# Regrouping the V rounds of a one-token attention kernel: waits between runs of rounds, and spare matmuls moved from the rounds to the tail

## The chip, the cores and the metric

One core of one Trainium2 chip. The metric is device time in microseconds of one execution; medians of several executions are given with their range, or with the interval of a ratio. "Span" is the time from the first to the last instruction of the profiled execution; it is about 1.4 us shorter than the time in most runs (2.8 us in the profiled run of the kernel before: 659.01 and 656.2).

## The reference, cut to what matters

One token (512 numbers) goes through layer norm, attention over a cache of 65,536 positions (8 K/V heads of 128, each serving 4 query heads), an output projection, a second layer norm and a gated feed-forward block, all in bf16:

```python
scores = jnp.einsum("bhqd,bhkd->bhqk", q, k) * (Dh ** -0.5)
p = _softmax(scores, axis=-1)
o = jnp.einsum("bhqk,bhkd->bhqd", p, v)
...
h = x + (o.transpose(0, 2, 1, 3).reshape(B, Sq, Hq * Dh) @ wo)
h2 = h + _B_ref(_layernorm(h), w_gate, w_up, w_down)
```

Everything is read once. K and V are 268.4 MB of the 282.33 MB that the profile counts, so this is a streaming kernel with little arithmetic for each byte.

## The kernel before

SyncE issues the loads, one after another on one queue, into a ring in SBUF. K of a head comes in three loads (12, 8 and 12 chunks of 512 KB), V the same. DVE transposes K's chunks, PE makes the scores, ACT the exponentials, and PE multiplies them with V in **rounds**: eight matmuls, 32 output rows each, on four column groups of the array. A head has a run of 10 rounds beside its first scoring block and one of 6 after its last. SyncE's loads wait for these rounds, because they free ring space:

```python
for h in range(1, HKV):
    load("K", h, 0, ["F0.1" if h == 1 else f"F{h - 1}.3"], "ka", f"K{h}.0")
    load("V", h - 1, 0, ["F0.3" if h == 1 else f"PV{h - 2}.3:2"], "va", f"V{h - 1}.0")
    load("V", h - 1, 1, ["F0.4" if h == 1 else f"PV{h - 2}.3"], "vb", f"V{h - 1}.1")
    load("K", h, 1, [f"F{h}.0"], "ka", f"K{h}.1")
    load("K", h, 2, [f"F{h}.1", f"PV{h - 1}.0:4"], "kb", f"K{h}.2")
    load("V", h - 1, 2, [f"PV{h - 1}.0"], "vb", f"V{h - 1}.2")
# ... last head: V7.0, output weights wo, V7.1, V7.2, V7.2b, gate, up, down weights
```

PE's program is a loop of registers and branches. This is the round (cut):

```python
label("values", "part")
e.reg_mov(m, PARTS[0])                 # 10 rounds; 6 in the last part
warm(e, 3)                             # three spare matmuls, results unused
# ...
goto("sums", "values")
pv_regs(e)                             # addresses of the round
# ...
away("br_eq", p, c, "waits", waits, "products")   # test in every round: time to wait for V?
goto("products", "sums")
section("B")                           # eight matmuls
mm_at(e, ps(5, 0, 504, 96, 128), ..., kept=True)  # the spare matmul of the round
# ... step p, v, m
e.br_ne(m, 0, on_true="sums", on_false="sums_end")
```

The waits for V's next piece stand off the loop ("away"): after 6 of the 10 rounds, and in the last head after 4 of the 6. Spare matmuls are there to keep PE's array busy and its granted clock up: the mean clock was 0.872 with them.

Of the kernel before, what the change touches and what calls it, by code (L numbers as in the profile page):

```python
# [10 lines left out]
ALU = mybir.AluOpType  # L11
# [15 lines left out]
PT_ROW = 4 * 512 + 8  # L27
# [8 lines left out]
class Prog:  # L36
# [14 lines left out]
    def op(self, eng, fn, deps=(), name=None, to=None, times=1):  # L51
        assert name is None or name not in self.where, name
        self.ops[eng].append(dict(fn=fn, deps=[d for d in deps if d], name=name, dma=None, to=to, times=times, part=self.part.get(eng)))
        if name:
            self.where[name] = (eng, len(self.ops[eng]) - 1)
# [160 lines left out]
def bass_sequential_preLN__gqa_block_cached__glu_gated_glu__decode_kernel(  # L216
# [21 lines left out]
    with ExitStack() as es:  # L238
        def sb(name, shape, dt):
            return es.enter_context(nc.sbuf_tensor(name, shape, dt))  # L240
# [18 lines left out]
        PT_sb = sb("PT_sb", [128, PT_ROW], bf16)  # L259
        qz = sb("qz", [128, 8 * 64], bf16)  # L260
# [39 lines left out]
        def ps(bank, c0, c1, p0=0, p1=128):  # L300
            return PS[p0:p1, bank * 512 + c0: bank * 512 + c1]
# [5 lines left out]
        op, dma = P.op, P.dma  # L307
# [98 lines left out]
        def addr_of(t, elements=0):  # L406
            return nc.lookup_mloc(t).addr + 2 * elements

        def at_reg(t, reg, ap):
            return mybir.RegisterAccessPattern(ap=ap, dtype=bf16, memsetref=t.name + "_set", regref=reg.name, is_regloc_offset=False,  # L410
                                               reg_ap_offset=reg.name, const_ap_offset=0, const_sub_tensor_id=0)

        def mm_at(e, out, lhsT, rhs, start, cols, col0=0, kept=False):
            more = dict(ldweights=False) if kept else {}
            return e.add_instruction(mybir.InstMatmult(  # L415
                name=nc.get_next_instruction_name(), engine=mybir.EngineType.PE, ins=[rhs, lhsT], outs=[e.lower_ap(out)],
                start_tensor_calc=start, stop_tensor_calc=False, tile_size=(128, cols), tile_position=(0, col0),
                bass_skip_group_check=True, **more))

        def warm(e, n=1, load=True):  # L420
            for i in range(n):
                more = dict(ldweights=False) if i or not load else {}
                e.add_instruction(mybir.InstMatmult(  # L423
                    name=nc.get_next_instruction_name(), engine=mybir.EngineType.PE, ins=[e.lower_ap(qz[:, 0:504]), e.lower_ap(ident[:, :])],
                    outs=[e.lower_ap(ps(5, 0, 504))], start_tensor_calc=True, stop_tensor_calc=True, tile_size=(128, 128),
                    tile_position=(0, 0), bass_skip_group_check=True, **more))

        regs, R, here = [], {}, OrderedEngineSet([mybir.EngineType.PE])
# [3 lines left out]
        def label(name, under=None):  # L432
            under = under or blocks[-1][0] if blocks else None
            parent = dict(blocks)[under] if under else "default"
            blocks.append((name, nc.switch_body(name, parent=parent, valid_engines=here)))

        def goto(name, under=None):
            nc.br(name, engines=here)
            label(name, under)

        def reg(e, i):
            while len(regs) <= i:
                regs.append(e.alloc_register(f"a{len(regs)}"))
            return regs[i]
# [133 lines left out]
        PARTS = {0: 10, 3: 6}  # L578
# [83 lines left out]
        def pe_flow(e, section):  # L662
            later = []

            def away(op, reg_, value, name, body, back=None):
                getattr(e, op)(reg_, value, on_true=name, on_false=f"{name}_not")
                later.append((name, body, back or f"{name}_not", blocks[-1][0]))
                label(f"{name}_not")

            i, w, p, v, m, c, s = (R.setdefault(n, e.alloc_register(f"r_{n}")) for n in "iwpvmcs")  # L670
            w0, p0 = addr_of(ktw, W0 + NC - 1 + 127), addr_of(PT_sb, 31 * 4)
            v_at = [addr_of(ring, j * CH) for j in AT["V"]]
            step = (2 * 2 * 512, 2 - 2 * 2 * 512)
            lag = v_at[0] - addr_of(ring, AT["V7"][0] * CH)
            i_last = v_at[0] - lag
            i_first = i_last + HKV * lag
            e.reg_mov(i, i_first)
            e.reg_mov(s, step[0])
            goto("head")
            e.reg_mov(w, w0)  # L680
            e.reg_mov(p, p0)
            e.reg_mov(c, p0 + 6)
            e.reg_alu(v, i, v_at[0], ALU.min)
            goto("part")
            e.br_eq(i, i_last, on_true="values", on_false="scores")
            label("scores")
            for half in range(NC // NR):
                for je in range(4):
                    if half or je:
                        e.reg_alu(reg(e, half * 4 + je), w, 2 * (je * WJ - half), ALU.add)  # L690
            away("br_eq", w, w0, "first_scores", lambda: section("As"), "more_scores")
            section("An")
            goto("more_scores", "scores")
            section("A")
            e.br_eq(i, i_first, on_true="next", on_false="values")
            label("values", "part")
            e.reg_mov(m, PARTS[0])
            warm(e, 3)
            away("br_eq", w, w0, "values0", lambda: section("V0"), "sums")
            e.br_ne(w, w0 - 12, on_true="next", on_false="values3")  # L700
            label("values3")
            e.reg_mov(v, v_at[2])
            e.reg_mov(m, PARTS[3])
            section("V3")
            goto("sums", "values")
            pv_regs(e)

            def last_second():
                section("L")

            def waits():
                e.reg_alu(c, c, 8, ALU.add)
                e.br_eq(w, w0, on_true="second", on_false="fourth")
                label("second", "waits")
                away("br_eq", i, i_last, "rows_of_o", last_second, "products")
                section("V2")
                nc.br("products", engines=here)
                label("fourth", "waits")
                e.br_ne(i, i_last, on_true="products", on_false="last_rounds")
                label("last_rounds", "fourth")  # L720
                section("VL")

            away("br_eq", p, c, "waits", waits, "products")
            goto("products", "sums")
            section("B")
            mm_at(e, ps(5, 0, 504, 96, 128), at_reg(PT_sb, reg(e, 11), [[PT_ROW, 128], [4, 32]]), e.lower_ap(qz[:, 0:504]), True, 32, 96, kept=True)
            e.reg_alu(p, p, s, ALU.add)
            e.reg_alu(s, s, step[0] ^ step[1], ALU.bitwise_xor)
            e.reg_alu(v, v, 2 * 2 * CH, ALU.add)
            e.reg_alu(m, m, -1, ALU.add)  # L730
            e.br_ne(m, 0, on_true="sums", on_false="sums_end")
            label("sums_end")
            def outs():
                warm(e, 2)
                section("O")
                warm(e, 1, load=False)

            away("br_eq", w, w0 - 12, "outs", outs)
            goto("next", "part")
            e.reg_alu(w, w, -4, ALU.add)  # L740
            e.br_ne(w, w0 - 16, on_true="part", on_false="head_end")
            label("head_end")
            e.br_eq(i, i_last, on_true="after", on_false="more_heads")
            label("more_heads")
            section("X")
            e.reg_alu(i, i, -lag, ALU.add)
            nc.br("head", engines=here)
            for name, body, back, under in later:
                label(name, under)
                body()  # L750
                nc.br(back, engines=here)
            label("after", "head_end")
# [44 lines left out]
        P.part = {}  # L797
        regroup(1)
        project(range(NQ - GS, NQ), O3, ["O3.1", "wo1"], last=True)
        op("pe", lambda e: warm(e, 1, load=False))  # L800


        ln_stats(1, lambda e: e.tensor_tensor(hT[1][:, :], ps(YT, 0, 4), x_col[:, :], ALU.add), "yT", STB, 0)
# [72 lines left out]
```

## Time and profile before

| | before |
|---|---|
| time, median of 6 runs | 657.81 us (657.55 to 658.58) |
| span of the profiled run | 656.2 us |
| PE, DVE, ACT busy | 460.9, 350.2, 42.9 us |
| mean granted clock of PE | 0.872 |
| transfer rate up to 653.6 us | 432 GB/s |

These are the lines on PE from the page: first busy time, share of the span and number of instructions for each engine; then three of the costliest groups, with busy time and mean ns of one before the second bar, and the engine's idle time ahead of them after it.

```profile
PE 460.9 (70%) x2564; PEld 73.8 (11%) x1587; DVE 350.2 (53%) x432; ACT 42.9 (7%) x114; POOL 3.6 (1%) x17
...
L415 PE MATMUL PS<-ring,PT_sb 128*32 x1024 | 90.5, 423 | 52.6 <-PEq L171 26.8
...
L415 PE MATMUL PS<-qz,PT_sb 128*32 128x504 bf16 x128 | 53.1, 415 | 0.0
...
L423 PE MATMUL PS<-qz,ident 128*128 128x504 bf16 x121 | 33.7, 374 | 2.1 <-issue 2.1
```

The reader is to see the 1024 V matmuls (128 rounds of 8), the 128 spare matmuls in the rounds, the 121 outside them: PE is busy for 70% of the span.

### The profile page before, as it was taken

What the parts mean: (1) busy time and instruction counts of PE and PEld (TensorE: products, weight loads), DVE (VectorE), ACT (ScalarE), POOL (GpSimd) and SP (SyncE); (2) the same over time, 40 slices, a digit from 0 to 9 for tenths busy, and PEclk for the clock granted to TensorE, in tenths of its full rate; (3) what the DMA queues carried; (4) which work ended last, traced back from release to release, by engine and by line L of the source; (5) the groups of instructions that cost most, each with busy time, mean ns of one, the idle gap of its engine ahead of it and who ended that gap; (6) DMA issues with size and microseconds to landing.
All of it is one profiled execution on the core that took longest, in us unless ns stands there. A gap on an engine that the chain in (4) does not pass through costs nothing.

```text
span 656.2 us, 6578 instructions
## 1 busy us (share of the span) xinstructions
PE 460.9 (70%) x2564; PEld 73.8 (11%) x1587; DVE 350.2 (53%) x432; ACT 42.9 (7%) x114; POOL 3.6 (1%) x17
## 2 busy tenths in 40 slices
PE   0688587857669567786677676695767966777776
PEld 0200010011001010010100111010100101001122
DVE  1299846747266645647258380684536572573202
ACT  1100200020000200001000200002000020001001
POOL 1000000000000000000000000000000000000000
PEclk9989799788889697896887988787978978879798
DMA  9999999999999999999999999999999999999998
GB/s 400 431 447 431 425 421 431 431 437 433 455 431 431 431 415 434 440 443 433 421 447 431 431 423 447 446 434 437 399 447 431 431 431 431 460 434 411 425 429 348
DMA packets 8498, 282.33 MB, mean 430 GB/s; under 512 B 1073, under 2 KB 1074, under 8 KB 1586
## 3 DMA queue, kind: packets, MB, share of 16 engines
q1 hardware_dynamic: 8354, 282.33, 99.6%
q10 hardware_dynamic: 144, 0.00, 0.0%
HBM read 282.33 MB, written 0.00 MB: 430 GB/s over the span
## 4 chain that ended last, share of the span: by engine, by line
DMA 54%; PE 26%; DVE 12%; issue 6%; ACT 1%; PEldq 0%; PEld 0%; SPq 0%
DMA ring<-in_A_k_cache_dram 33%; PE PS L415 22%; DMA ring<-in_A_v_cache_dram 19%; DVE ktw L504 11%; DMA x_col<-in_A_x_dram 2%; PE PS L423 2%; ACT P_sb L550 1%; PE PS L817 0%; DVE PT_sb L560 0%; DVE M_sb L511 0%; PE PS L660 0%; PEldq L171 0%; PE PS L835 0%; PE PS L386 0%; PE PS L544 0%
## 5 line engine op out<-in xcount | busy, mean ns | idle before, releaser
L504 DVE STREAM_TRANSPOSE ktw<-ring 128x1024 f32<-128x1024 f32 x256 | 292.3, 1207 | 152.2 <-DMA ring<-in_A_k_cache_dram 152.2
L415 PE MATMUL PS<-ktw 128*128 128x512 bf16 x1024 | 287.1, 430 | 103.2 <-DVE ktw L504 86.0
L415 PE MATMUL PS<-ring,PT_sb 128*32 x1024 | 90.5, 423 | 52.6 <-PEq L171 26.8
L415 PEld LDWEIGHTS PS<-ktw 128*128 x256 | 26.7, 104 | 343.6 <-issue 246.4
L415 PE MATMUL PS<-qz,PT_sb 128*32 128x504 bf16 x128 | 53.1, 415 | 0.0
L415 PEld LDWEIGHTS PS<-ring,PT_sb 128*32 x1024 | 25.0, 115 | 134.7 <-issue 131.0
L593 ACT ACTIVATE po_sb<-PS,rl 128x512 bf16<-128x512 f32 x8 | 5.5, 687 | 524.1 <-PE PS L415 524.1
L423 PE MATMUL PS<-qz,ident 128*128 128x504 bf16 x121 | 33.7, 374 | 2.1 <-issue 2.1
L511 DVE TENSOR_REDUCE M_sb<-PS 128x1 f32<-128x512 f32 x32 | 19.9, 683 | 22.4 <-PE PS L415 22.4
L539 DVE TENSOR_REDUCE gmj<-PS 1x4 f32<-1x128 f32 x8 | 2.2, 279 | 46.0 <-PE PS L537 46.0
L550 ACT ACTIVATE P_sb<-PS,negmax 128x512 bf16<-128x512 f32 x32 | 21.6, 686 | 0.3
L560 DVE STREAM_TRANSPOSE PT_sb<-P_sb 128x512 bf16<-128x512 bf16 x32 | 20.1, 680 | 1.5 <-ACT P_sb L550 1.5
L386 PE MATMUL PS<-st,onesf 128*128 128x2 f32 x4 | 1.0, 312 | 17.1 <-DVE st L385 17.1
L415 PE MATMUL PS<-ring,xz 128*8 x32 | 9.6, 471 | 2.3 <-issue 2.3
L609 DVE TENSOR_TENSOR Lw<-O,blk_of 128x896 bf16<-128x896 bf16 (+1 forms) x2 | 1.4, 683 | 17.7 <-ACT O L599 17.7
L567 DVE TENSOR_REDUCE lsum<-PS 128x1 f32<-128x4 f32 x8 | 1.3, 162 | 17.6 <-PE PS L565 17.6
L415 PE MATMUL PS<-ktw,O 128*1 x26 | 7.5, 377 | 0.6
L423 PEld LDWEIGHTS PS<-qz,ident 128*128 128x128 bf16 x40 | 3.8, 96 | 35.3 <-issue 35.3
L544 PE MATMUL PS<-one_f,gmrep 1*128 1x1 f32 x16 | 3.2, 268 | 5.0 <-DVE gmrep L541 5.0
L468 DVE STREAM_TRANSPOSE qt<-qh 32x512 bf16<-32x512 bf16 x1 | 0.7, 700 | 11.0 <-ACT qh L465 11.0
L401 DVE CAST hT<-x_col 128x4 f32<-128x4 bf16 x1 | 0.2, 170 | 11.9 <-DMA x_col<-in_A_x_dram 11.9
L550 ACT ACTIVATION_READ_ACCUMULATOR P_sb<-PS,negmax 128x1 f32 x32 | 6.5, 203 | 0.0
(85 smaller groups left out, 73.9 us busy)
## 6 DMA issues: line engine op xcount, KB each, us to landing
ring<-in_A_k_cache_dram SPq DMA_DIRECT2D x16, 6144.0 KB, 24.4
ring<-in_A_v_cache_dram SPq DMA_DIRECT2D x15, 6144.0 KB, 24.9
ring<-in_A_v_cache_dram SPq DMA_DIRECT2D x9, 4096.0 KB, 29.6
ring<-in_A_k_cache_dram SPq DMA_DIRECT2D x8, 4096.0 KB, 24.7
ring<-in_A_wq_dram SPq DMA_DIRECT2D x1, 4096.0 KB, 12.3
ktw<-in_A_wo_dram SPq DMA_DIRECT2D x1, 3584.0 KB, 13.1
ring<-in_A_v_cache_dram SPq DMA_DIRECT2D x1, 2048.0 KB, 36.8
ring<-in_B_w_gate_dram SPq DMA_DIRECT2D x1, 1792.0 KB, 28.4
```

What stands on the lines that cost most here:

```text
L386: op("pe", lambda e: e.matmul(ps(bank, c0, c0 + 2), lhsT=onesf[:, :], rhs=st[i][:, :], start=True, stop=True), [f"st.{i}", f"sta.{i}", "on ...
L415: return e.add_instruction(mybir.InstMatmult(name=nc.get_next_instruction_name(), engine=mybir.EngineType.PE, ins=[rhs, lhsT], outs=[e.low ...
L423: e.add_instruction(mybir.InstMatmult(name=nc.get_next_instruction_name(), engine=mybir.EngineType.PE, ins=[e.lower_ap(qz[:, 0:504]), e.lo ...
L504: op("dve", lambda e, d=dst, sr=src: e.transpose(d, sr), deps, f"T{b}.{c}", to="T")
L511: op("dve", lambda e, u=u: e.tensor_reduce(M_sb[:, u % 4:u % 4 + 1], ps(u % NS, 0, 512), AX.X, ALU.max), [f"S{b}.{NC - NR + k}"], f"mx{u}" ...
L539: op("dve", lambda e: e.tensor_reduce(gmj[:, :], ps(MISC, 0, 128, 0, 1).rearrange("p (i a c) -> p a i c", a=4, c=NC), AX.XY, ALU.max), [f" ...
L544: op("pe", lambda e: e.matmul(ps(MISC, 128, 129), lhsT=gmrep[0:1, :], rhs=one_f[0:1, 0:1], start=True, stop=True), [f"gmrep{h}"], f"neg{h}")
L550: op("act", lambda e, b=b: e.activation(P_sb[:, (b % 4) * 512:(b % 4 + 1) * 512], ps(b % NS, 0, 512), AF.Exp, bias=negmax[:, k:k + 1], sca ...
L560: op("dve", lambda e, b=b: e.transpose(PT_sb[:, (b % 4) * 512:(b % 4 + 1) * 512], P_sb[:, (b % 4) * 512:(b % 4 + 1) * 512]), [f"E{b}"], f" ...
L567: op("dve", lambda e: e.tensor_reduce(lsum[:, :], ps(MISC, 132, 136), AX.X, ALU.add), [f"l{h}"], f"ls{h}", to="D")
L593: op("act", lambda e: e.activation(po_sb[:, :], ps(PO, 0, 512), AF.Copy, scale=rl[:, :]), [f"PV{h}.{NR - 1}", f"rl{h}"], f"po{h}", to="po")
L609: op("dve", lambda e: e.tensor_tensor(Lw[i][:, :].rearrange("p (j c) -> p j c", j=n), bass.AP(tensor=O2, offset=j0, ap=[[NQ, 128], [1, n], ...
```

## The change

Its intent: a round costs PE's sequencer a test and a jump (0.10 to 0.15 us by runs 2 and 5 below) that matter only twice a head. So the rounds are put in runs (6 then 4, and 4 then 2), with the wait between the runs; the spare matmul leaves the round; the parts keep two spares instead of three, and two places in the tail get one more.

```diff
-            e.reg_mov(m, PARTS[0])
-            warm(e, 3)
+            e.reg_mov(m, 6)
+            e.reg_mov(k, 4)
+            warm(e, 2)
 ...
-            e.reg_mov(m, PARTS[3])
+            e.reg_mov(m, 4)
+            e.reg_mov(k, 2)
 ...
             def waits():
-                e.reg_alu(c, c, 8, ALU.add)
+                e.reg_alu(m, k, 0, ALU.add)
+                e.reg_mov(k, 0)
 ...
-            away("br_eq", p, c, "waits", waits, "products")
-            goto("products", "sums")
             section("B")
-            mm_at(e, ps(5, 0, 504, 96, 128), ..., kept=True)
 ...
             e.br_ne(m, 0, on_true="sums", on_false="sums_end")
             label("sums_end")
+            away("br_ne", k, 0, "waits", waits, "sums")
 ...
-                warm(e, 1, load=False)          # after a head's outputs
+                warm(e, 2, load=False)
 ...
-        op("pe", lambda e: warm(e, 1, load=False))   # tail, before the second layer norm
+        op("pe", lambda e: warm(e, 2, load=False))
```

More of the change, by code (lines that the diff above doesn't have):

```diff
@@ L668, in away @@
                 label(f"{name}_not")
-            i, w, p, v, m, c, s = (R.setdefault(n, e.alloc_register(f"r_{n}")) for n in "iwpvmcs")
+            i, w, p, v, m, k, s = (R.setdefault(n, e.alloc_register(f"r_{n}")) for n in "iwpvmks")
             w0, p0 = addr_of(ktw, W0 + NC - 1 + 127), addr_of(PT_sb, 31 * 4)
@@ L681, in pe_flow @@
             e.reg_mov(p, p0)
-            e.reg_mov(c, p0 + 6)
             e.reg_alu(v, i, v_at[0], ALU.min)
@@ L711, in waits @@
             def waits():
-                e.reg_alu(c, c, 8, ALU.add)
+                e.reg_alu(m, k, 0, ALU.add)
+                e.reg_mov(k, 0)
                 e.br_eq(w, w0, on_true="second", on_false="fourth")
                 label("second", "waits")
-                away("br_eq", i, i_last, "rows_of_o", last_second, "products")
+                away("br_eq", i, i_last, "rows_of_o", last_second, "sums")
                 section("V2")
-                nc.br("products", engines=here)
+                nc.br("sums", engines=here)
                 label("fourth", "waits")
-                e.br_ne(i, i_last, on_true="products", on_false="last_rounds")
+                e.br_ne(i, i_last, on_true="sums", on_false="last_rounds")
                 label("last_rounds", "fourth")
                 section("VL")
-            away("br_eq", p, c, "waits", waits, "products")
-            goto("products", "sums")
             section("B")
-            mm_at(e, ps(5, 0, 504, 96, 128), at_reg(PT_sb, reg(e, 11), [[PT_ROW, 128], [4, 32]]), e.lower_ap(qz[:, 0:504]), True, 32, 96, kept=True)
             e.reg_alu(p, p, s, ALU.add)
```

## The prediction

Passages of the recorded text are cut, and each cut is marked: figures and rules of the hardware that no trace or run of this case shows, and a remark on the transfer rate. One is a term of the round's sum, what I took for the test and the jump. With it and the 0.03 us for the spare the sum came to 0.19 us a round, 24 us in all; it stands as my estimate, and so do the numbers that rest on it (0.95 us a round, 3 us in the last head, 1.4 us at the eviction). For the figures of the second rival the trace of the kernel before has: scoring matmuls start 0.43 us apart at a granted clock of 0.50 (77.55 to 81.82 us) and 0.22 us apart at 1.00; the eight matmuls of a round start in two groups of four (639.70 and 639.94 us); eight transposes take 9.13 us (from 529.75 us).

> **What bounds the kernel now.** I read the page's slices and DMA totals first, then the loads from issue to landing, then the last microseconds in stretches, and the rounds that the change edits last.
>
> From the page, slices of DMA share and GB/s and the total:
>
> ```profile
> DMA  9999999999999999999999999999999999999998
> DMA packets 8498, 282.33 MB, mean 430 GB/s; under 512 B 1073, under 2 KB 1074, under 8 KB 1586
> ```
>
> The queue has no slack slice. Split where the data ends (columns: stretch, its length, PE, PEld, DVE, ACT, POOL busy with counts, clock, DMA share, GB/s):
>
> ```profile
> 0.00:653.60 653.60, 460.25 (x2536) 73.43 (x1563) 349.69 (x430) 42.35 (x112) 3.59 (x17) 0.87 1.00 432
> 653.60:656.20 2.60, 0.66 (x44) 0.41 (x32) 0.56 (x2) 0.54 (x2) 0.00 (x0) 0.98 0.00 0
> ```
>
> For 653.6 us the engines run at share 1.00 and 432 GB/s, and only 2.6 us follow. 282.33 MB / 432 GB/s is 653.5 us: the transfers are the time. The chain of waits hides this a little, because it credits PE and DVE with pieces that run beside transfers; it still gives DMA most:
>
> ```profile
> DMA 54%; PE 26%; DVE 12%; issue 6%; ACT 1%; PEldq 0%; PEld 0%; SPq 0%
> ```
>
> Next, whether PE can starve the queue. PE's V rounds release ring space, so loads wait for them. From issue to landing:
>
> ```profile
> ring<-in_A_k_cache_dram SPq DMA_DIRECT2D x16, 6144.0 KB, 24.4
> ring<-in_A_v_cache_dram SPq DMA_DIRECT2D x15, 6144.0 KB, 24.9
> ring<-in_A_v_cache_dram SPq DMA_DIRECT2D x9, 4096.0 KB, 29.6
> ring<-in_A_k_cache_dram SPq DMA_DIRECT2D x8, 4096.0 KB, 24.7
> ...
> ktw<-in_A_wo_dram SPq DMA_DIRECT2D x1, 3584.0 KB, 13.1
> ```
>
> At 432 GB/s a load of 6144 KB needs 14.6 us itself, 4096 KB 9.7 us, 3584 KB 8.5 us. So at its issue there lay ahead of it, as an estimate from these medians, 9.8, 10.3, 19.9, 15.0 and, at the thinnest place (the first output weights, issued at 602.50), 4.6 us of other transfers. A load issued earlier only stands longer in line. DVE waits 152.2 us for K in all, 19 us a head: compute, too, has slack in each head.
>
> Last, the end. The last weights are three loads issued at 618.23, 618.70 and about 619.17, landing after 33.9, 34.6 and 34.8 us: at 652.1, 653.3 and 654.0. The last 56 matmuls use 32, 16 and 8 of their instructions on these three. Weight loads of that line in stretches of 0.05 us (columns: stretch, length, PEld busy and count, clock, DMA share, GB/s):
>
> ```profile
> 653.80:653.85 0.05, 0.05 (x8) 1.00 0.00 0
> 653.85:653.90 0.05, 0.05 (x4) 1.00 0.00 0
> 653.90:653.95 0.05, 0.00 (x1) 1.00 0.00 0
> 653.95:654.00 0.05, 0.03 (x8) 1.00 0.00 0
> 654.00:654.05 0.05, 0.05 (x8) 1.00 0.00 0
> ```
>
> The stream, some 9 active in each stretch, pauses at 653.90 to 653.95 and resumes with exactly eight: the last eight waited for the last load. The chain view calls this whole group PE work behind DVE, but the pause says that the last landing, not PE, sets the end already.
>
> [...] no record shows one branch, only the gaps in which they lie. [...] granted clock 1.00 at 640 to 649 with spare matmuls in every round, 0.50 at 650 to 652.
>
> **The change part by part.** There are 16 V rounds a head (10 in one run, 6 in another), 128 in all. One late round in the trace:
>
> ```profile
> 639.70 0.63 PE L415 MATMUL PS<-ring,PT_sb 128*32 x8 [0.32 <-issue]
> 640.16 0.38 PE L415 MATMUL PS<-qz,PT_sb 128*32 128x504 bf16 x1
> 640.81 0.63 PE L415 MATMUL PS<-ring,PT_sb 128*32 x8 [0.27 <-issue]
> ```
>
> The period is 1.11 to 1.17 us; the eight real matmuls with their loads and the spare are handed over in the first 0.46 us, and the rest is register work and branches. The idle is put down to issue: a round is bound by PE's sequencer, not by the array.
>
> - Removed per round: the spare matmul (about 0.03 us of issue by 17 instructions in 0.46 us; 0.84 - 0.63 = 0.21 us of array time), one compare-and-branch and one jump [...]. Estimate: 1.13 becomes about 0.95 us, so 0.19 x 128 = 24 us less PE time in all.
> - Moved: the test for a wait now stands after a run of 6 or 4 rounds. The runs are 6+4 and 4+2, just where the counter's test fired before (after 6 of 10, and after 4 of the other 6), so each wait covers the same data. The detour stays: the gap before the round at 642.85 was 1.19 us against about 0.3, and I leave its 0.9 us in.
> - Removed per part: one of three spare matmuls, 32 times, about 0.21 us each of array time. Added: one more after each head's output (8) and one in the tail (1), about 0.2 us each, under waits of PE for ACT and DVE. Spare matmuls of that line go from 121 to 64 + 32 + 2 = 98.
> - Array busy time: 460.9 - 128 x 0.21 - 23 x 0.21 = about 429 us if the clock holds.
>
> Of the 24 us, the seven heads before the last give nothing: earlier releases lengthen the line at the queue. In the last head 16 rounds x 0.19 is 3 us at most. There V's pieces land, by issue plus time to landing, at about 626.5, 636 and 641.1 us, queued long before and untouched by PE. I expect the last V rounds to stand at the wait for 641.1 for a moment, so that the final eviction, at 644.72 before, starts near 643.3: some 1.4 us gained. Then the gate and up weights (last piece at 617.75 + 31.9 = 649.7) hold their last matmuls, and finally the down weights' last piece at 654.0 holds the last eight. From there the same path remains: eight matmuls, two evictions, the output's transfer. Sum on the path that sets the end: 0.0 us, perhaps a few hundredths.
>
> **The rivals.**
> First, the tail's compute as the bound. For it: the chain view ends in PE and DVE, with 26% PE, and some 1.4 us could come off; it would give about 656.4. Against it: the pause before the last eight matmuls and 432 GB/s up to 653.6. A few tenths could come from it at most if the landing were not quite what ended the pause.
>
> Second, the clock. Without spares the array may [...] fall to half clock. A round of eight matmuls in two groups of four would then take about 2 x 0.43 = 0.86 us of array time, still under the 0.95 of the sequencer. The scoring matmuls after them could suffer: 32 a block at 0.43 us would be 13.8 us against DVE's 8 transposes of about 1.14 us, 9.1 us. If every block ran cold, 4 x 4.7 = 19 us a head would use up all of DVE's 19 us wait, and the queue could run dry: several us to over 2% slower. Against it: DVE's pace already leaves PE waiting in scoring blocks at 0.50 clock today, and spares remain at both ends of each run. I give this 3% for anything visible.
>
> Third, a faster PE sends loads earlier and the transfers interfere with one another or with compute. All loads but one come from one queue and line up; I see no new meeting. This leaves the time alone.
>
> Fourth, a wait that takes the removed one's place: exactly what I expect in the last head (641.1, 649.7, 654.0). It makes the time the same and is the mechanism of my number.
>
> **Range and chances.** The central value is the median before, 657.8, less 0.1 us for the odd hundredths: I choose 657.7. The three runs before span 657.55 to 658.43, and the profiled one took 659.01[...]. So 8 in 10: 656.9 to 658.7. Faster by over 2% needs 13.2 us less, below what 282.33 MB takes at the measured rate: 0.3%. Slower by over 2% needs the clock rival in full: 0.7%. Within 2%: 99%.
>
> **What would show it.** If I am right, the profile after has the same 432 GB/s to about 653.5 us; rounds with a period of 0.9 to 1.0 us and one group of 8 matmuls each; PE busy near 430 us; longer times to landing for the big loads (a queue more ahead of its data); the last eviction 1 to 2 us earlier; pauses in the last 56 matmuls, before the sixteen and before the last eight, of about 1 us together, and the eight's start again near 654.0. The round's step is wrong if the period stays above 1.05 us or falls under 0.8. The clock step is wrong if the mean granted clock falls from 0.872 to under 0.75. The prediction as a whole is wrong if the data ends more than 1 us from 653.6, or if less than 2.3 us or more than 3 us pass from the end of data to the end of the span.

## The result, and the profile after

The changed kernel took 657.91 us (median of 6, 657.46 to 659.24), the kernel before 657.81 us in the same rounds. The ratio is 1.0002, 95% interval 0.9989 to 1.0015: the same. (Ratios are the mean time of one kernel's runs over that of the other's of the same rounds, so not quite the ratio of the medians quoted.)

PE did less. From the page of the changed kernel, the engines and the same groups (the spares of the rounds are gone):

```profile
PE 447.5 (68%) x2413; PEld 71.4 (11%) x1587; DVE 350.3 (53%) x432; ACT 42.8 (7%) x114; POOL 3.6 (1%) x17
...
L415 PE MATMUL PS<-ring,PT_sb 128*32 x1024 | 95.8, 475 | 61.7 <-PEq L171 36.1
...
L423 PE MATMUL PS<-qz,ident 128*128 128x504 bf16 x98 | 33.2, 426 | 3.8 <-issue 3.8
```

There are 151 matmuls fewer (128 and 23), but a V matmul is recorded at 475 ns instead of 423: the mean granted clock fell from 0.872 to 0.822. Busy time fell by 13.4 us only.

The transfers did not change. Slices and total of the page, then the two stretches (columns as in the prediction):

```profile
DMA  9999999999999999999999999999999999999998
...
DMA packets 8499, 282.33 MB, mean 430 GB/s; under 512 B 1074, under 2 KB 1075, under 8 KB 1587
```

```profile
0.00:653.60 653.60, 446.92 (x2397) 71.18 (x1575) 349.79 (x430) 42.31 (x112) 3.58 (x17) 0.82 1.00 432
653.60:656.40 2.80, 0.60 (x24) 0.23 (x24) 0.56 (x2) 0.54 (x2) 0.00 (x0) 0.74 0.01 5
```

Where the earlier releases went shows in the time from a load's issue to its landing:

```profile
ring<-in_A_v_cache_dram SPq DMA_DIRECT2D x15, 6144.0 KB, 25.2
ring<-in_A_v_cache_dram SPq DMA_DIRECT2D x9, 4096.0 KB, 29.9
...
ktw<-in_A_wo_dram SPq DMA_DIRECT2D x1, 3584.0 KB, 14.4
```

V's loads stand 0.3 us longer in line than before (24.9 and 29.6), the output weights 1.3 us longer (13.1). They were issued earlier and landed when the queue came to them.

In the last head the gain turns into waits. PE's rounds of the last part in the timeline of the changed kernel (start, duration; in brackets the idle time before and what ended it). The first line is four rounds in one piece, the next three are the weight loads of the second to the fourth of them, the last is the fifth round:

```profile
636.96 4.01 PE L415 MATMUL PS<-ring,PT_sb 128*32 x32 [1.53 <-PEq L171]
637.92 0.16 PEld L415 LDWEIGHTS PS<-ring,PT_sb 128*32 x8 [0.81 <-issue]
638.94 0.16 PEld L415 LDWEIGHTS PS<-ring,PT_sb 128*32 x8 [0.86 <-issue]
639.91 0.16 PEld L415 LDWEIGHTS PS<-ring,PT_sb 128*32 x8 [0.81 <-issue]
...
641.88 0.63 PE L415 MATMUL PS<-ring,PT_sb 128*32 x8 [0.91 <-DMA ring<-in_A_v_cache_dram]
```

A round takes 0.97 to 1.02 us instead of 1.11 to 1.17. PE stands ahead of the six rounds: from the start of the four rounds before them (628.38) to 636.96 it took 8.58 us, against 7.28 us (628.14 to 635.42) in run 4, where these pieces of V land before 630 us. Here the piece of 4096 KB landed at about 636.4 (issue at 602.73 plus 33.7). At the fifth round nothing is lost, although its line names a landing: from the start of the fourth it took 1.97 us (639.91 to 641.88), and in run 4, with no landing to wait for, 1.96 us (638.38 to 640.34). The last 56 matmuls, which ran in one piece with one hitch before, now come in three:

```profile
652.41 0.62 PE L836 MATMUL PS<-ring,hhT 128*1 128x128 bf16 x32 [1.22 <-DMA ring<-in_B_w_down_dram]
653.53 0.39 PE L836 MATMUL PS<-ring,hhT 128*1 128x128 bf16 x16 [0.50 <-DMA ring<-in_B_w_down_dram]
654.15 0.28 PE L836 MATMUL PS<-ring,hhT 128*1 128x128 bf16 x8 [0.23 <-DMA ring<-in_B_w_down_dram]
```

Each group of 32, 16 and 8 waits for its own load of the down weights. The last eight start at 654.15 us, against about 653.97 before.

The clock shows best in the four rounds ahead of V's last piece. The stretch in the kernel before:

```profile
637.40:641.70 4.30, 3.38 (x36) 0.66 (x32) 0.00 (x0) 0.00 (x0) 0.00 (x0) 1.00 1.02 436
```

and in the changed kernel:

```profile
636.90:641.00 4.10, 4.01 (x32) 0.64 (x32) 0.00 (x0) 0.00 (x0) 0.00 (x0) 0.50 1.02 436
```

In the kernel before PE was busy for 3.38 of 4.30 us at full clock. In the changed kernel it was busy for 4.01 of 4.10 us at half clock: fewer matmuls, more "busy". This is why busy time alone tells little of PE. The pair does not show that the missing spares did this: the same four rounds ran at 1.00 without a spare in runs 2 and 6 (busy for 2.53 us in both), and at 0.63 with it in run 1. What decides the clock of one such stretch is open.

### The profile page after: what moved, and what is told of

The parts are those of the page before. It is cut to its first block, busy times and chain, and to the rows that moved or that the text cites. A ratio compares the mean times of both kernels' runs of the same rounds, so it can differ in the third digit from the quotient of the medians.

```text
span 656.4 us, 6378 instructions
## 1 busy us (share of the span) xinstructions
PE 447.5 (68%) x2413; PEld 71.4 (11%) x1587; DVE 350.3 (53%) x432; ACT 42.8 (7%) x114; POOL 3.6 (1%) x17
## 4 chain that ended last, share of the span: by engine, by line
DMA 60%; PE 22%; DVE 13%; issue 3%; ACT 1%; SPq 0%; PEldq 0%
DMA ring<-in_A_k_cache_dram 34%; PE PS L415 20%; DMA ring<-in_A_v_cache_dram 19%; DVE ktw L504 12%; DMA ring<-in_B_w_down_dram 6%; DMA x_col<-in_A_x_dram 2%; PE PS L423 1%; ACT P_sb L550 1%; DVE PT_sb L560 0%; DVE M_sb L511 0%; SPq L350 0%; PE PS L537 0%; SPq L355 0%; PE PS L565 0%; PEldq L171 0%
## 5 line engine op out<-in xcount | busy, mean ns | idle before, releaser
L415 PE MATMUL PS<-ktw 128*128 128x512 bf16 x1024 | 290.6, 434 | 107.9 <-DVE ktw L504 92.2
L415 PE MATMUL PS<-ring,PT_sb 128*32 x1024 | 95.8, 475 | 61.7 <-PEq L171 36.1
L415 PEld LDWEIGHTS PS<-ring,PT_sb 128*32 x1024 | 21.1, 117 | 131.1 <-issue 129.5
L401 DVE CAST hT<-x_col 128x4 f32<-128x4 bf16 x1 | 0.2, 171 | 12.1 <-DMA x_col<-in_A_x_dram 12.1
L537 PE MATMUL PS<-identf,gm 128*1 128x128 f32 x16 | 4.1, 348 | 2.2 <-DVE gm L535 2.1
## 6 DMA issues: line engine op xcount, KB each, us to landing
ring<-in_A_k_cache_dram SPq DMA_DIRECT2D x16, 6144.0 KB, 24.3
ring<-in_A_k_cache_dram SPq DMA_DIRECT2D x8, 4096.0 KB, 24.6
```

Source lines behind the costliest of these rows:

```text
L415: return e.add_instruction(mybir.InstMatmult(name=nc.get_next_instruction_name(), engine=mybir.EngineType.PE, ins=[rhs, lhsT], outs=[e.low ...
L537: op("pe", lambda e: e.matmul(ps(MISC, 0, 128, 0, 1), lhsT=gm[:, :], rhs=identf[:, :], start=True, stop=True), [f"gm{h}"], f"gmT{h}", to="Q")
```

## The experiments

My theory: the transfers set the time in every head and at the end; what PE gains is real, but is spent standing in line or waiting for landings. Rivals: (a) PE gained nothing, because the lower clock gave all of it back; (b) rounds lie on the path, and two effects cancel. Each kernel is compared with the kernel before in the same rounds.

**1. The runs alone, with the spare put back.**

```diff
             section("B")
+            mm_at(e, ps(5, 0, 504, 96, 128), ..., kept=True)
```

> The changed kernel with the spare matmul put back into every V round: the runs of rounds alone, without the test. Transfers as the bound: same time as both kernels, 657 to 659 us. Round period: the spare costs only its issue, so about 1.03 us against 1.00 in the changed kernel and 1.13 in the old one. Clock: if the spare is what held the clock up, the mean granted clock is back near 0.87 (0.822 in the changed kernel); if it is the test or the tail, it stays near 0.82.

Measured: 658.46 us against 657.60, ratio 1.0010 (0.9996 to 1.0025): the same. The clock is 0.847, half way back from 0.822 to 0.872; what gives the other half was not tested. Two rounds after a wait started 1.00 us apart.

**2. The spare alone taken out of the old round.**

```diff
-            mm_at(e, ps(5, 0, 504, 96, 128), ..., kept=True)
```

> The kernel before with only the spare matmul taken out of the round; the test in every round stays. Transfers as the bound: 657 to 659 us. Round period about 1.10 us (1.13 less the issue of one matmul). Clock: near 0.82 if the spare held it up, near 0.87 if not. Rival (PE's rounds on the path): a time between the two, by some tenths.

Measured: 658.14 us, ratio 1.0008 (0.9994 to 1.0023): the same. The clock is 0.807. Rounds start at 636.87, 638.02, 639.18 and 640.29, 1.14 us apart: not the 1.10 expected, and no shorter than with the spare (1.13). So the test and its jump are what shortened the round, and the spare is what held the mean clock up (0.872 to 0.807 here, 0.847 to 0.822 from run 1 to the changed kernel). Neither moved the time.

**3 and 4. Both kernels with 12 us of transfers taken from the end.** Ten of the last twelve chunks of V in the last head are not loaded (the result is wrong), so everything behind them lands 12.1 us earlier:

```diff
-            load("V", h, 2, (), ("vb", "vl")[i], f"V{h}.2{('', 'b')[i]}", cols)
+            load("V", h, 2, (), ("vb", "vl")[i], f"V{h}.2{('', 'b')[i]}", (cols[0], cols[0] + 1))
```

> The kernel before with ten of the last head's twelve last chunks of V not loaded (5120 KB, wrong result on purpose): everything behind them lands 5.24 MB / 432 GB/s = 12.1 us earlier. If the last landing alone set the end and compute were far ahead, 12 us less. My theory: in the kernel before compute stood only some 0.1 us ahead of the last landing, so the time hardly falls: 0 to 0.5 us less, 657.3 to 658 us, and the last 56 matmuls run without a pause.

> The changed kernel with the same 5120 KB not loaded (wrong result on purpose). My theory: the change did make the last head's compute faster and the landings hid it; with them gone the saving shows: last eviction near 642.3 us instead of 643.6, no wait for the last V piece, no pauses in the last 56 matmuls, time 2 to 3 us less than the changed kernel and than the kernel before cut in the same way (about 655.3 us). Rival (slower clock gave the saving back): same time as the cut kernel before, within 0.5 us.

Measured, kernel before: 658.23 us, ratio 1.0006 (0.9993 to 1.0018). Twelve microseconds of transfers less at the end, and nothing gained: its compute ended level with the last landing. The stretch from 640 to 645 us and the last matmuls of the cut kernel before:

```profile
640.00:645.00 5.00, 3.19 (x33) 0.58 (x25) 0.00 (x0) 0.60 (x1) 0.00 (x0) 1.00 0.28 111
```

```profile
653.36 0.95 PE L835 MATMUL PS<-ring,hhT 128*1 128x128 bf16 x56 [1.13 <-DVE hhT L830]
```

The transfers run out between 640 and 645 us (share 0.28), and all 56 matmuls start in one piece as soon as DVE has their input.

Measured, changed kernel: 656.45 us (655.37 to 658.01), ratio 0.9987 (0.9975 to 0.9999). From the two ratios it is 0.9987 / 1.0006 = 0.9981, or 1.2 us, ahead of the kernel before cut in the same way; from the two intervals I estimate 0.1 to 2.4 us. The profiled spans are 654.1 and 656.2; the traced execution is one of the two fastest of its six (655.49 us). The gain does not rest on this run alone: three more cut variants of the changed kernel (runs 5, 6 and 8) lie 2.2 to 3.2 us ahead of the cut kernel before, by their ratios. The same matmuls:

```profile
651.22 0.95 PE L836 MATMUL PS<-ring,hhT 128*1 128x128 bf16 x56 [1.29 <-DVE hhT L831]
```

They start 2.14 us earlier than in the kernel before cut alike. This is the gain that the whole kernel hides, so rival (a) falls in part: something was gained. It is less than the 2 to 3 us I expected of the time. Compare the first output matmuls of the last head: they run from the head before's to the last head's in 645.14 - 602.82 = 42.32 us in the one and 642.91 - 602.24 = 40.67 us in the other, 1.65 us less. The first six rounds with what stands around them saved 1.28 us of this (7.59 to 6.31), the last six 0.58 us (7.40 to 6.82); the four in between saved nothing (3.63 us in both), most likely because the array, at a granted clock of 0.59 there against 1.00 in the cut kernel before, takes 0.8 us a round (3.15 us for the four) and became their bound.

**5. The cut changed kernel with the spare back in every round.** The edits of 1 and 3 on the changed kernel.

> The changed kernel with the spare matmul back in every round and the last head's V cut by 5120 KB as in the two cut kernels before (wrong result on purpose), so that compute sets the end. If the spare held the clock and the clock was worth something: the four rounds after the row products at clock 1.00 take 0.3 to 0.4 us less than in the cut changed kernel (3.63 us to the part's first spare there), and the time is equal to that kernel's (656.45 us) or up to 0.7 us less. If the spare costs more than the clock gives: 0.3 to 1 us more than that kernel.

Measured: 655.17 us (654.74 to 656.04), ratio 0.9958 (0.9945 to 0.9972), some 1.9 us (0.9987 - 0.9958 = 0.29%) ahead of the cut changed kernel without it. That is more than the 0.7 us I allowed for, and not where I expected it: the four rounds still took 4.25 us (627.48 to 631.73), with their clock low (0.67). The clearest difference is in the tail. The gate and up matmuls of the cut changed kernel, then of this one:

```profile
646.50 3.02 PE L818 MATMUL PS<-ring,hc 128*1 128x448 bf16 x32 [0.26 <-DVE hc L805]
```

```profile
646.15 1.69 PE L819 MATMUL PS<-ring,hc 128*1 128x448 bf16 x32 [0.25 <-DVE hc L806]
```

3.02 us at a granted clock of 0.58 from 645 to 650, 1.69 us at 1.00. This does not account for the 1.9 us. The last 56 matmuls started only 0.68 us earlier (650.54), and the two profiled executions took 655.49 and 655.33 us, 0.16 us apart: the difference of the means comes from slower executions of the cut changed kernel (up to 658.01 us) that left no trace. Nor is the slow stretch a cost of the change, for the kernel before, cut alike, has it too:

```profile
648.50 3.16 PE L817 MATMUL PS<-ring,hc 128*1 128x448 bf16 x32 [0.26 <-DVE hc L804]
```

So of rival (a) only the four rounds of run 4 are left; that the lower clock cost exposed compute more than this is not shown. In the whole kernel (run 1) no gain of the spare shows in the time.

**6. The cut changed kernel with the old tail**, one spare in place of two after the outputs and before the layer norm.

```diff
-                warm(e, 2, load=False)
+                warm(e, 1, load=False)
 ...
-        op("pe", lambda e: warm(e, 2, load=False))
+        op("pe", lambda e: warm(e, 1, load=False))
```

> The changed kernel with the last head's V cut by 5120 KB, and one spare instead of two after the outputs and in the tail, as before the change. If the two added spares matter to exposed compute, it is 0.3 us or more slower than the cut changed kernel (656.45 us, 655.37 to 658.01); if they fill waits without moving the clock, the same within its spread.

Measured: 655.81 us (655.11 to 656.73), ratio 0.9972 (0.9958 to 0.9985), not slower than with the two added spares (0.9987; the intervals overlap). The gate and up matmuls took 3.12 us, against 3.02 us with them: as slow. The two spares added in the tail did not hold the clock up there.

**7. No spare matmul at all**, `warm(e, 0)` everywhere.

> The changed kernel without any spare matmul, in parts, around the outputs and in the tail. The granted clock falls below 0.822, I guess to 0.65 to 0.75. My theory: DVE's 19 us of waiting a head and the 10 us of transfers ahead of each load hide it in the heads; in the last head it slows compute by about the 1 us of pauses that it had, so 657.5 to 659 us. Rival (the clock is what the spares buy, and the queue runs dry without them): over 662 us, and a transfer rate under 428 GB/s.

Measured: 657.64 us against 657.62, ratio 0.9996 (0.9981 to 1.0011): the same, with 249 matmuls fewer than the kernel before and a clock of 0.80 (I guessed lower). Its last head shows work done early, then waiting:

```profile
627.12 3.90 PE L415 MATMUL PS<-ring,PT_sb 128*32 x32 [2.25 <-DMA ring<-in_A_v_cache_dram]
636.81 4.01 PE L415 MATMUL PS<-ring,PT_sb 128*32 x32 [5.78 <-PEq L171]
...
653.97 0.28 PE L835 MATMUL PS<-ring,hhT 128*1 128x128 bf16 x8 [0.23 <-DMA ring<-in_B_w_down_dram]
```

(Of the 5.78 us, 4.13 us are there in run 8 too, where V has landed long before.) The last eight matmuls start at 653.97 us, where the kernel before has them. The spares, which hold the mean clock up, buy nothing while transfers set the time.

**8. The same without spares, cut at the end as in 3.**

> No spare matmul at all, with the last head's V cut by 5120 KB so that compute sets the end (wrong result on purpose). Whole, this kernel took 657.64 us and waited for four landings in the last head. If those waits hid work done early, the cut shows it: the end some 3 us or more before 656.2 in the profile, 652 to 655 us. If spares are worth something to exposed compute, it is slower than the cut kernel with a spare in each round (655.17 us).

Measured: 655.60 us (655.20 to 656.47), ratio 0.9970 (0.9956 to 0.9983). The hidden lead is there again, 2.3 us by the spans (656.2 to 653.9), less than the 3 us I expected; against the cut kernel with a spare in each round (0.9958) the intervals overlap. It is not slower than the cut changed kernel (0.9987) either, at a mean clock of 0.788 and with gate and up matmuls of 3.15 us: here, too, the lower clock shows no cost in the time.

**9. Six spares in every round.**

```diff
             section("B")
+            for _ in range(6):
+                mm_at(e, ps(5, 0, 504, 96, 128), ..., kept=True)
```

> The changed kernel with six spare matmuls in each V round, which makes a round about 1.7 us instead of 1.0: 128 x 0.7 = 90 us more of PE time. My theory: in seven heads the 11 us each are hidden; only the last head's 16 rounds lie on the path once they pass the landings: about +10 us, 665 to 669 us, with 432 GB/s up to the last load. Rival (rounds on the path in every head): +40 us and more. If everything is hidden in the last head too: under 659 us.

Measured: 671.64 us (669.08 to 672.47), ratio 1.0195 (1.0174 to 1.0215). Rounds are 1.70 us apart and PE is busy 547.5 us, 100 us more than in the changed kernel. The stretches of this kernel:

```profile
0.00:653.60 653.60, 538.05 (x3054) 97.00 (x1472) 345.84 (x415) 40.82 (x109) 3.03 (x16) 0.92 1.00 432
653.60:667.00 13.40, 9.49 (x128) 4.14 (x115) 4.45 (x17) 2.03 (x5) 0.55 (x1) 0.73 0.04 15
```

The rate of the transfers is that of the other kernels, and they end about half a microsecond later (15 GB/s over 13.4 us are 0.2 MB). So the 112 slower rounds of the seven heads before the last cost half a microsecond at most; nearly all of the 10.7 us on the span (656.4 to 667.1) comes from the last head's 16, of about the size expected. The time lay above the 665 to 669 us expected. Rival (b) falls: rounds lie on no path before the last head. The time rose by 3 us more than the span did: it exceeds the span by 4.8 to 5.4 us here, against 1.4 us in most runs (and 2.8 us in the profiled run of the kernel before). What those 3 us are no view shows; they stay open.

**10. 4096 KB of V less in the middle**, at head 3:

```diff
-            load("V", h - 1, 2, [f"PV{h - 1}.0"], "vb", f"V{h - 1}.2")
+            load("V", h - 1, 2, [f"PV{h - 1}.0"], "vb", f"V{h - 1}.2", (20, 24) if h == 4 else None)
```

> The changed kernel with 4096 KB of head 3's V not loaded, in the middle of the run (wrong result on purpose). Transfers as the bound everywhere: 4.19 MB / 432 GB/s = 9.7 us less, 648 us. Rival (compute is the bound in the heads and transfers only follow it): less than 2 us less.

Measured: 651.52 us, 6.1 us less, ratio 0.9907 (0.9892 to 0.9922). That is neither theory's number. The stretch in which the rate fell:

```profile
350.00:354.00 4.00, 3.46 (x9) 0.25 (x2) 4.00 (x5) 0.00 (x0) 0.00 (x0) 0.50 0.64 205
```

The next head's first K load is issued at 350.84, when DVE has passed a chunk of K that landed at 346.17. The V load that I cut is what kept the queue busy meanwhile; cut to a third it no longer reached. That left a hole, by my reading of my own making: the K load then landed 17.8 us after issue instead of 24.2.

**11. The same kind of cut in small portions**, to test that reading: 1024 KB in each of six heads.

```diff
+            ... f"V{h - 1}.2", (20, 30) if h < 7 else None)
```

> The changed kernel with 1024 KB of V's last piece not loaded in each of six heads (wrong result on purpose), where the run before left out 4096 KB in one place and got 6.1 us instead of 9.7, with the rate at 205 GB/s for some 4 us after the gap. If that hole was the missing cover of one load and transfers are the bound in every head, small cuts leave the cover whole and the time falls by all of 6.29 MB / 432 GB/s = 14.6 us, to 643 to 644 us. If compute sets the pace of the heads in part, it falls by clearly less, under 12 us.

Measured: 643.78 us against 657.65, 13.9 us less by the medians and 14.1 by the ratio of 0.9785 (0.9770 to 0.9800), of 14.6 expected. Bytes taken out of the heads come out of the time almost in full, as long as no load's cover is taken away. Compute set no part of the pace that one could see.

No experiment points to a version that beats both kernels: the bytes are the least that can be read, the rate is 432 GB/s from nearly the first microsecond to 653.6, and what follows the last landing (eight matmuls, two evictions, the output) is the same in both.

## Why the prediction was right

The time on record was 657.7 us, the measured one 657.91, within the range. By its steps:

- *Transfers are the time.* Right: 432 GB/s up to 653.6 us in both kernels, and in the ones without spares and with six. That the stream itself can give no more than this was not shown: no run tried to raise the rate. Runs 9 and 11 show it from both sides: rounds of 1.70 us in place of 0.99 put half a microsecond at most on seven heads, 6.29 MB less took 14 us off.
- *The last landing, not PE, sets the end.* Right, with a nuance that run 3 added: in the kernel before, compute and landing ended level, so "not PE" was too strong. Taking only the transfers away gained nothing; taking only PE's work away (the change) gained nothing; both together gained 1.2 us by run 4, and 2.2 to 3.2 us by the variants of runs 5, 6 and 8.
- *The round, 1.13 to 0.95 us.* Mis-sized a little: about 0.99 us, so 128 x 0.14 = 18 us of rounds in place of 24. The term taken for the test and the jump was too large: runs 2 and 5 against their partners give 0.10 to 0.15 us for the pair. For the spare they give -0.01 to 0.04 us, which the 0.03 us taken for it fits.
- *The last head.* Its eviction at 643.59 (643.3 foretold, 644.72 before). The wait that was foretold at V's last piece (641.1) came one piece earlier, at about 636.4, and cost 1.3 us (8.58 against 7.28 us in run 4); at the last piece PE waited no longer than without a landing. Then pauses of 0.50 and 0.23 us before the sixteen and the eight (about 1 us together foretold; the idle of the weight loads there is 0.69 and 0.42); the eight at 654.15 (near 654.0).
- *PE busy time, about 429 us if the clock holds.* Wrong in its condition: 447.5 us. The clock did not hold (0.822), a V matmul is recorded 12% longer. The clock rival had been given 3% "for anything visible": visible in the records it was, in the time it was not, because the heads have slack and the last head waits. What makes the clock fall is not shown: the trace has the two clocks, but before the fall to 0.50 at 649 to 650 us PE never stood idle for more than 1.19 us from 637.4 us on.
- *Longer times to landing for the big loads.* Right for V (0.3 us) and the output weights (1.3 us), not for K (24.4 to 24.3 and 24.7 to 24.6).

Not settled: the 3 us between span and time in run 9, and most of what the spare in each round was worth in run 5.

## What to carry to other kernels

Before an engine's work is made cheaper, look for what released the last instructions, and count how much other traffic stands ahead of each load at its issue: work that only frees buffers for a queue that is never empty can be made faster or slower by many microseconds without a trace in the time (here 18 us less of rounds in all left the ratio at 1.0002, and some 80 us more in seven heads, 112 rounds of 1.70 in place of 0.99 us, cost half a microsecond at most). When two chains end level, removing either one alone shows nothing (ratios of 1.0006 in run 3 and 1.0002 for the change), so an experiment that is to show the hidden gain must take the other away. And do not read a busy share as a load: at half clock fewer matmuls were more busy (32 for 4.01 us at 0.50, 36 for 3.38 us at 1.00).

## What the runs show of PE's clock, and what stays open

- The granted clock was 1.00 or 0.50, with means between them where a stretch holds both. What makes it fall is open: rounds of 8 matmuls every 0.99 us ran at 0.50 for 4 us in the changed kernel and at 1.00 in run 6; in the kernel before the clock fell at 649 to 650 us after 11.6 us in which PE was busy for 7.76 us and never idle for more than 1.19 us. Mean clocks were 0.80 with no spares at all, 0.822 with two to four at the ends of the runs, 0.847 with one in each round, 0.872 with the old set and 0.92 with six.
- The same loop of two matmuls a pass (26 in all, output projection) took 8.07 us in the kernel before and 8.20 in the changed one, but 5.77 without spares and 5.78 with six in each round (8.50 with one in each round, run 1). The clock alone does not order these (it was 1.00 there in the kernel before). The loop was hidden behind landings here; its cause is open.
